# One decode pass fewer per weight tile, and new due times for W2's decode

## The chip, the cores and the metric

The kernel runs on one core of a Trainium2 chip. The metric is the time of one execution on the device in microseconds (us), as the median of several runs. Three runs of the kernel before took 1174.15, 1174.5 and 1177.13 us: median 1174.5.

## The reference

The arrays q, k and v are float32; the four weight matrices are float64. What is computed, with B = 4 batches, H = 8 heads, S = 576 positions, D = 64:

```
q, k   = rotary embedding of q, k
x      = softmax(q k^T / 8) v                      # 2304 x 512 after the heads are joined
h      = x @ w_in                                  # layer 1 (moe): 512 -> 2048
x      = (h * clip(h + 3, 0, 6) / 6) @ w_out       #                2048 -> 512
h      = x @ w_in2                                 # layer 2 (moe2): 512 -> 2048
P      = a0 + a1 h + a2 h^2 + a3 h^3
Q      = 1 + |b0| |h| + |b1| h^2
out    = (P / (Q + 1e-6)) @ w_out2                 #                2048 -> 512
```

## The kernel before

The weights of both layers arrive as 64-bit floats, seen as pairs of 32-bit integers, low word and high word (`raw`, 128 x 512 x 2). A **decode** makes one 128 x 512 float32 tile of them. There are 16 tiles for each of the four matrices: layer 1's (W1, 32 tiles, `prep_w1i` and `prep_w1o`) and layer 2's (W2, 32 tiles, `prep_w2`). A decode has these passes over 512 elements a partition: the high word, read as a float, is scaled by 2^-112, which rebases its exponent (line 557, on GpSimd or ScalarE, in the early part on VectorE or ScalarE; it shows under the helper's lines 449, 451 and 455); a shift left by 3 (L559, VectorE); the sign bit of the high word is put back in (L561, VectorE); the top bits of the low word are put in below (L565, VectorE). For the last 6 tiles of W1's first matrix the sign comes another way: ScalarE takes Sign of the high word (L564) and GpSimd multiplies by it at the end (L568).

W1's decoded tiles are bounded (Square with a sum, L582), scaled and split into two float16 parts that add up to them (lines 449 and 574). W2's decoded tiles, one `f32` buffer for all of them, are written to a scratch tensor `w2d` in device memory (L642) and read back when layer 2 begins.

**Phase 1** holds attention and layer 1. Attention works in 144 chunks of 128 queries, 36 to a batch: scores `s` (L762), their maximum `mx` (L766, scaled at L767), the exponential `e` (L772), its float16 part and residue `p` (lines 449 to 453, L779, L780), a transposing DMA to `pt` (L784), and the product with v into `ob` (L792). Each batch feeds layer 1 in two parts, with a product `h` (L859), the passes over `t` (L863, L865), the float16 parts `gh` and `gl` (L868), and the second product (L883). **Phase 2** is layer 2, in five blocks of up to 512 tokens (L1046 to L1079). It takes over the memory of attention, and then that of layer 1 and the decodes, so all W2 decodes end before its elementwise passes can begin.

The order of the instructions is the work of a **planner** (`Plan.order`). Each operation has a list of engines that may do it, a cost on each, and a due time as its priority. The planner walks through a modelled time, and at each step gives an engine that is free the ready operation with the smallest due time. A ready operation is not held back for its due time: an engine with nothing more urgent takes it. Due times are counted in ticks, one tick for a chunk. W2's 32 tiles are due evenly between `w20` and `w21`:

```
    for z in range(2 * KF):
        at(PR["w20"] + z * (PR["w21"] - PR["w20"]) / (2 * KF))
        prep_w2(z // KF, z % KF)
```

Of the kernel before, what the change touches and what calls it, by code (L numbers as in the profile page):

```python
# [10 lines left out]
F32 = mybir.dt.float32  # L11
# [4 lines left out]
AF = mybir.ActivationFunctionType  # L16
ALU = mybir.AluOpType
# [6 lines left out]
D = 64  # L24
# [6 lines left out]
KF = DFF // 128  # L31
# [7 lines left out]
PR = {'c01': -12.75,  # L39
 'e': 2,  # L40
 'e_dec': 'GA',
 'e_dec0': 'DA',
 'e_gh': 'GA',
 'e_gh0': 'AD',
 'e_gl': 'DG',
 'e_gl0': 'D',
 'e_hi': 'D',
# [118 lines left out]
 'tick': 4000,  # L166
 'u': 2,
 'vv': 1,
 'w20': 48.25,
 'w21': 163,  # L170
 'w2h': 'A',
 'w2l': 'DG',
 'wg': 4,
# [59 lines left out]
def cls(nm):  # L233
    for x in ("ob", "xu", "sm", "xt", "v9", "w0_", "w1_", "w2_", "acc"):
        if nm.startswith(x):
            return x
    return nm


def two(e):  # L240
    return float(2.0 ** e)
# [20 lines left out]
class Plan:  # L262
# [11 lines left out]
    def op(self, engs, cost, fn, r=(), w=(), lat=None, prio=None):  # L274

        o = Op()
        o.engs, o.fn, o.deps, o.idx = engs, fn, set(), len(self.ops)
        ww = [x[0] if isinstance(x, tuple) else x for x in w]; rr = [x[0] if isinstance(x, tuple) else x for x in r]
        o.nm = (">" + ww[0].tag) if ww else ("<" + rr[0].tag if rr else "?")
        o.dma = cost if type(cost) is tuple else None  # L280
        o.cost = cost if type(cost) is dict else {e: cost for e in engs}
        o.prio, o.lat = self.prio if prio is None else prio, lat
        o.prio += PR.get("o_" + cls(o.nm[1:]), 0) * 4000
        if self.first:
            o.prio += PR.get("z_" + cls(o.nm[1:]), 0) * 4000
        for writes, keys in ((False, r), (True, w)):
            for key in keys:
                t, part = key if isinstance(key, tuple) else (key, None)
                if isinstance(t, Til):
                    t.ops.append(o)  # L290
                    self.used.setdefault(t.pool, []).append(o)
                for p_, (wr, rd) in t.last.items():
                    if p_ is None or part is None or p_ == part:
                        o.deps.update(wr)
                        if writes:
                            o.deps.update(rd)
                if writes:
                    if part is None:
                        t.last.clear()
                    t.last[part] = ([o], [])  # L300
                else:
                    t.last.setdefault(part, ([], []))[1].append(o)
        o.deps.discard(o)
        self.ops.append(o)
        return o
# [99 lines left out]
def c_act(n, ap=0, sbuf=True, acc=False):  # L405
    return n / 1.2 + 51 + 42 * sbuf + 93 * ap + 190 * acc


def c_dve(n, ap=0):
    return n * 1.042 + 68 + 60 * ap  # L410


def c_dve2(n, ap=0):
    return n * 0.521 + 68 + 60 * ap


def c_copy(n, ap=0, sbuf=True):
    return {"A": c_act(n, ap, sbuf), "D": c_dve2(n, ap) if sbuf else c_dve(n, ap), "G": n * (0.9 + 0.14 * ap) + 124}


def c_sub(n):
    return {"D": c_dve(n), "G": c_pool(n)}
# [6 lines left out]
def c_pool(n):  # L429
    return n * 2.17 + 125  # L430
# [7 lines left out]
def attention_moe_moe2(ctx, tc, q, k, v, w1i, w1o, w2i, w2o, a, b, tabs, out):  # L438
# [4 lines left out]
    vec, act, pool, pe, sp = nc.vector, nc.scalar, nc.gpsimd, nc.tensor, nc.sync  # L443
    DE = {"Q": sp, "A": act}
    EL = {"D": vec, "G": pool, "A": act}

    def copy(e, out, in_, scale=1.0):
        if e == "A":
            act.activation(out, in_, AF.Copy, scale=scale)  # L449
        elif e == "G":  # L450
            pool.tensor_scalar(out, in_, scale, 0.0, ALU.mult, ALU.add)
        elif isinstance(scale, float) and scale == 1.0:
            vec.tensor_copy(out, in_)  # L453
        else:
            vec.tensor_scalar(out, in_, scale, None, ALU.mult)
    ctx.enter_context(tc.manual_schedule())
    pl = Plan()
    op, tl = pl.op, pl.tile

    def EN(key):  # L460
        return PR.get(key + "0", PR[key]) if pl.early else PR[key]
# [55 lines left out]
    def pow2(src, src_ap, n, target, nm, pool_name, inv=None, inv_ap=None):  # L517

        pi = tl(pool_name, [128, n], I32, nm + "i", 2)
        sc = tl(pool_name, [128, n], F32, nm + "s", 4)  # L520
        if inv is None:
            inv = tl(pool_name, [128, n], F32, nm + "v", 4)
            inv_ap = inv
        op("D", 75, lambda e: vec.tensor_scalar(pi(), src_ap().bitcast(I32), 1, 0x3F800000, ALU.logical_shift_right,
                                                ALU.bitwise_and), r=[src], w=[pi])
        op("D", 75, lambda e: vec.tensor_scalar(inv_ap(), pi().bitcast(F32), two(-124), two(64 - target), ALU.max,
                                                ALU.mult), r=[pi], w=[inv])
        op("D", 85, lambda e: vec.reciprocal(sc(), inv_ap()), r=[inv], w=[sc])
        return sc, inv


    def load_raw(src, is_in, f):
        t = tl("right", [128, 512, 2], I32, "raw", PR["raw"])
        w = src.bitcast(I32)

        def fn(e):
            if is_in:
                DE[e].dma_start(out=t().rearrange("p (k n) two -> p k (n two)", k=KD),
                             in_=w[:, f * 256:(f + 1) * 256].rearrange("(k p) n -> p k n", p=128))
            else:  # L540
                DE[e].dma_start(out=t().rearrange("p n two -> p (n two)"), in_=w[f * 128:(f + 1) * 128])
        op(PR["q_raw"], (450, 1456), fn, w=[t])
        return t

    def decode(t, f, sg=None):

        def lo():  # L550
            return t()[:, :, 0]

        def hi():
            return t()[:, :, 1]

        def fi():
            return f().bitcast(I32)
        op(EN("e_dec"), c_copy(512), lambda e: copy(e, f(), hi().bitcast(F32), two(-112)), r=[t], w=[f])
        op("D", c_dve2(512), lambda e: vec.tensor_single_scalar(fi(), fi(), 3, op=ALU.logical_shift_left), w=[f])  # L559
        if sg is None:  # L560
            op("D", c_dve(512), lambda e: vec.scalar_tensor_tensor(fi(), hi(), -2 ** 31, fi(), ALU.bitwise_and,  # L561
                                                                   ALU.bitwise_or), r=[t], w=[f])
        else:
            op("A", c_act(512), lambda e: act.activation(sg()[:, 0], hi().bitcast(F32), AF.Sign), r=[t], w=[(sg, 0)])  # L564
        op("D", c_dve(512), lambda e: vec.scalar_tensor_tensor(fi(), lo(), 29, fi(), ALU.logical_shift_right,  # L565
                                                               ALU.bitwise_or), r=[t], w=[f])
        if sg is not None:
            op(EN("e_sg"), c_sub(512), lambda e: EL[e].tensor_tensor(f(), f(), sg()[:, 0], ALU.mult), r=[(sg, 0)], w=[f])  # L568

    w1 = [[None] * KF for _ in range(2)]  # L570

# [5 lines left out]
    def bound(dst, dst_ap, src, n, by=1.0, src_ap=None):  # L577

        def fn(e):
            x = (src_ap or src)()  # L580
            dims = "a b c"[:2 * len(x.shape) - 3]
            act.activation(junk[:, 0:n], x.rearrange(f"p {dims} -> p ({dims})"), AF.Square, scale=by,  # L582
                           accum_out=dst_ap())
        op("A", c_act(n, 0, True, True), fn, r=[src], w=[dst])

    def total(am, am_ap, n, kind=0):
        ps, ps_ap = small(128, n, kind)
        op("P", 60, lambda e: pe.matmul(ps_ap(), lhsT=ones(), rhs=am_ap(), start=True, stop=True), r=[ones, am], w=[ps])
        return ps, ps_ap

    WG = PR["wg"]

    def prep_w1i(g):

        am = tl("right", [128, WG], F32, "wam", 2)
        fts = []
        for i in range(WG):
            raw = load_raw(w1i, True, g * WG + i)
            ft = tl("right", [128, 512], F32, f"w1_{(g * WG + i) % (KF - 1)}", 1)
            t = tl("right", [128, 2, 512], F16, f"w0_{g * WG + i}")  # L600
            w1[0][g * WG + i] = t
            decode(raw, ft, t if g * WG + i >= KF - PR["sg"] else None)
            bound((am, i), lambda i=i: am()[:, i:i + 1], ft, 512)
            fts.append(ft)
        ps, ps_ap = total(am, am, WG, 1)
        gs = slice(g * WG, g * WG + WG)
        sc, _ = pow2(ps, ps_ap, WG, 14, "wp", "right", (pwi, g), lambda: pwi()[:, gs])
        for i in range(WG):
            split16(w1[0][g * WG + i], fts[i], sc, lambda i=i: sc()[:, i:i + 1])
# [363 lines left out]
    def to_right(e):  # L973
# [15 lines left out]
       w=[(ab, 0)])  # L989
    op("Q", (450, 56), lambda e: DE[e].dma_start(out=ab()[:, 4:6], in_=b.rearrange("(o n) -> o n", o=1).to_broadcast([128, 2])),  # L990
       w=[(ab, 1)])
# [187 lines left out]
```

## Time and profile before

| What | us | Share of the span |
|---|---|---|
| median of three runs | 1174.5 | |
| the profiled execution, its time | 1176.04 | |
| the profiled execution, its span | 1174.3 | |
| TensorE (PE) busy | 978.5 | 83% |
| VectorE (DVE) busy | 1012.9 | 86% |
| ScalarE (ACT) busy | 693.6 | 59% |
| GpSimd (POOL) busy | 536.2 | 46% |

A row of a group gives the line, the engine, the operation, the tiles (out<-in, without buffer numbers), the shape and the count, then the busy time in us and the mean duration of one in ns, then the idle time of the engine just before these instructions and what ended most of it. Instructions of one engine overlap a little at their ends, so that count times mean can exceed the busy time. Names that begin with w are W1's tiles and the parts made of them, and f is the f32 buffer, which holds W2's tiles and the last tile of W1's second matrix.

### The profile page before, as it was taken

The numbers are of one execution on the slowest core, as the hardware profiler recorded it, in microseconds if no ns is written. First come the engines' busy times: TensorE is split into PE (matmuls) and PEld (weight loads), VectorE is DVE, ScalarE is ACT, GpSimd is POOL, SyncE is SP. The second block draws the span as 40 slices with busy tenths as digits, with TensorE's granted clock in tenths as the row PEclk, the third lists the DMA queues.
The fourth block names the chain that finished last, engine by engine and source line by source line (L and its number), as shares of the span: only waits on it lengthen the run. The fifth ranks groups of instructions, "written<-read, shape, count | busy, mean of one in ns | idle before, by whom it ended". The sixth has DMA issues, their size and how long they took to land.

```text
span 1174.3 us, 20041 instructions
## 1 busy us (share of the span) xinstructions
PE 978.5 (83%) x7030; PEld 756.6 (64%) x7030; DVE 1012.9 (86%) x1920; ACT 693.6 (59%) x1274; POOL 536.2 (46%) x603
## 2 busy tenths in 40 slices
PE   0222469887888889988899999989999999999997
PEld 0111247755566666666666787767888888888885
DVE  7999989799899998899978955489988887888787
ACT  5555668475455354453444526478776675676576
POOL 5799778687588857699843620035000000000000
PEclk9999989999999999899999999999999999999999
DMA  8788877787887897978869651622020020010010
GB/s 237 184 219 178 218 145 156 152 175 163 189 177 157 154 220 187 191 149 161 188 165 196 145 127 33 197 83 76 1 61 3 19 54 1 5 41 1 1 37 18
DMA packets 297445, 142.73 MB, mean 122 GB/s; under 512 B 245120, under 2 KB 278528, under 8 KB 297344
## 3 DMA queue, kind: packets, MB, share of 16 engines
q1 hardware_dynamic: 286352, 123.72, 48.8%
q10 hardware_dynamic: 10992, 17.73, 5.3%
q8 instruction: 55, 0.90, 0.3%
q14 instruction: 46, 0.38, 0.1%
HBM read 61.71 MB, written 17.83 MB: 68 GB/s over the span
## 4 chain that ended last, share of the span: by engine, by line
PE 42%; DVE 28%; DMA 8%; issue 6%; POOL 6%; ACT 4%; SPq 1%; ACTq 0%; DVEq 0%; POOLq 0%
PE ac L1079 14%; PE hh L1046 8%; PE hx L1046 7%; PE h L883 6%; PE h L859 5%; DMA pt<-p 4%; DVE mx L766 3%; DVE gl L868 2%; DVE p L453 2%; DVE t L865 2%; DMA w2d<-f 2%; DMA raw<-in_moe_w_out_dram 2%; DVE qk L732 1%; ACT e L772 1%; PE s L762 1%
## 5 line engine op out<-in xcount | busy, mean ns | idle before, releaser
L859 PE MATMUL h<-xt,w 128*128 128x256 f16 (+1 forms) x1536 | 207.6, 289 | 31.8 <-DVE t L865 27.4
L859 PEld LDWEIGHTS <-w 128*128 128x128 f16 x1536 | 149.2, 99 | 73.9 <-issue 36.9
L883 PE MATMUL h<-gh,w 128*128 128x256 f16 (+1 forms) x960 | 195.8, 290 | 0.5 <-DVE w L574 0.4
L772 ACT ACTIVATE e<-s,mx,qal 128x576 f32<-128x576 f32 x144 | 118.7, 827 | 122.8 <-DVE mx L767 37.5
L1079 PE MATMUL ac<-w,lgh 128*128 128x512 f32 x576 | 180.1, 393 | 4.8 <-ACT lgh L1069 4.0
L779 POOL TENSOR_TENSOR p<-e,p 128x512 f16<-128x512 f32 x104 | 138.9, 1335 | 64.6 <-DVE p L453 42.5
L883 PEld LDWEIGHTS <-w 128*128 128x128 f16 x1440 | 139.5, 99 | 36.3 <-DVE w L574 0.7
L883 PE MATMUL h<-gl,w 128*128 128x256 f16 (+1 forms) x480 | 139.2, 290 | 0.0
L762 PE MATMUL s<-t,t 128*128 128x512 f16 (+2 forms) x320 | 89.6, 313 | 55.1 <-ACT e L772 48.2
L792 PE MATMUL ob<-v,pt 128*128 128x130 f16 (+3 forms) x1440 | 96.3, 217 | 45.2 <-DMA pt<-p 19.3
L762 PEld LDWEIGHTS <-t 128*128 128x128 f16 (+1 forms) x640 | 59.0, 108 | 107.2 <-issue 68.4
L1079 PEld LDWEIGHTS ac<-w,lgh 128*128 128x128 f32 x576 | 106.8, 188 | 30.6 <-ACT lgh L1069 6.6
L1046 PE MATMUL hh<-x,w 128*128 128x512 f32 (+1 forms) x516 | 115.9, 373 | 2.9 <-DVE lt L1061 2.9
L792 PEld LDWEIGHTS <-pt 128*128 128x128 f16 (+1 forms) x1440 | 81.5, 105 | 55.4 <-issue 26.4
L1079 PE MATMUL ac<-w,lgl 128*128 128x512 f32 x288 | 113.6, 394 | 1.2 <-DVE lgl L1070 1.2
L766 DVE TENSOR_REDUCE mx<-s 128x1 f32<-128x576 f32 x144 | 107.0, 745 | 6.8 <-PE s L762 6.6
L1046 PEld LDWEIGHTS hh<-x,w 128*128 128x128 f32 x516 | 90.9, 188 | 23.0 <-DVE lt L1061 3.8
L1046 PE MATMUL hx<-x,w 128*128 128x512 f32 (+1 forms) x444 | 98.2, 370 | 0.0
L863 ACT ACTIVATE t<-h,half,d 128x256 f32<-128x256 f32 (+1 forms) x128 | 74.7, 585 | 26.9 <-PE h L859 25.7
L1046 PEld LDWEIGHTS hx<-x,w 128*128 128x128 f32 x444 | 77.4, 188 | 16.1
L868 DVE TENSOR_TENSOR gl<-t,gh 128x256 f16<-128x256 f32 (+1 forms) x108 | 69.2, 643 | 12.1 <-ACT gh L449 11.0
L449 ACT ACTIVATE gh<-t 128x256 f16<-128x256 f32 (+1 forms) x95 | 41.6, 440 | 51.1 <-DVE t L865 48.8
(151 smaller groups left out, 2088.8 us busy)
## 6 DMA issues: line engine op xcount, KB each, us to landing
raw<-in_moe_w_in_dram SPq DMA_DIRECT2D x32, 512.0 KB, 4.8
raw<-in_moe_w_out_dram SPq DMA_DIRECT2D x32, 512.0 KB, 4.5
w2d<-f ACTq DMA_DIRECT2D x30, 256.0 KB, 3.7
w2s<-w2d SPq DMA_DIRECT2D x22, 256.0 KB, 2.7
out_dram<-ob SPq DMA_DIRECT2D x36, 128.0 KB, 2.4
nat<-in_k_dram SPq DMA_DIRECT2D x16, 256.0 KB, 3.2
nat<-in_q_dram SPq DMA_DIRECT2D x16, 256.0 KB, 3.2
vnat<-in_v_dram SPq DMA_DIRECT2D x4, 1024.0 KB, 7.6
```

Of the source, the lines that this page charges most:

```text
L449: act.activation(out, in_, AF.Copy, scale=scale)
L762: pe.matmul(s()[r0:r0 + m, c:c + n_], lhsT=qq[:, q0:q0 + m], rhs=kk[:, k0:k0 + n_], start=(j == 0), stop=(j == 1))
L766: op("D", c_dve(576), lambda e: vec.reduce_max(mx()[:, 0:1], s()[:, 0:S], axis=AX.X), r=[s], w=[(mx, 0)])
L772: op("A", c_act(576, 2, False), lambda e: act.activation(et(), s()[:, 0:S], AF.Exp, bias=mx()[:, 1:2], scale=al()[:, 0:1]), r=[s, (mx, 1), ...
L779: EL[e].tensor_tensor(p16()[:, S + 64:2 * S], et()[:, 0:512], p16()[:, 0:512], ALU.subtract)
L792: pe.matmul(ob()[0:m, o0:o0 + c], lhsT=pt()[:, j, q0:q0 + m], rhs=v9()[:, hh, j % 5].rearrange("p s d -> p (s d)")[:, 0:c], start=(n_ == 0 ...
L859: pe.matmul(hp()[:, 0:N], lhsT=w[:, z, kk], rhs=xt()[:, kk, 0:N], start=(n == 0), stop=(n == 11))
L863: op("A", c_act(N, 2, False), lambda e, t=t, hp=hp, f=f: act.activation(t()[:, 0:N], hp()[:, 0:N], AF.Relu, bias=half(), scale=d()[:, f:f ...
L868: op(EN("e_gl"), c_sub(N), lambda e, t=t, f=f: EL[e].tensor_tensor(gl()[:, f, 0:N], t()[:, 0:N], gh()[:, f, 0:N], ALU.subtract), r=[t, (gh ...
L883: pe.matmul(yp()[:, 0:N], lhsT=w[:, s_, m * 128:(m + 1) * 128], rhs=gt()[:, f, 0:N], start=(f == 0 and z == 0), stop=(f == KF - 1 and z == 2))
L1046: pe.matmul(hp()[:, 0:n], lhsT=w[:, kk], rhs=xt()[:, kk, 0:n], start=(i == 0), stop=(i == 11))
L1079: pe.matmul(accs[j][i]()[0:m], lhsT=gt()[:, x:x + m], rhs=wt(), start=(f == 0 and z == 0), stop=(f == KF - 1 and z == 2))
```

## The change

There are two edits. First, in the decode the scaling becomes a Prelu on ScalarE in all 64 tiles. For a positive high word it scales by 2^-112 as before. For a negative one it multiplies by the slope -2^32 besides: the value turns positive, and its exponent field is larger by 32, which is the bit that the shift left by 3 then moves into the sign's place. So the pass that put the sign back (L561) is gone, and with it the other way of six tiles (L564, L568). Second, the due times of W2's decodes run from tick 112 to 165 instead of 48.25 to 163. Lines behind the decode have numbers that are 11 smaller in the changed kernel.

```
- 'w20': 48.25,
- 'w21': 163,
+ 'w20': 112.0,
+ 'w21': 165.0,
...
-    def decode(t, f, sg=None):
+    def decode(t, f):
...
-        op(EN("e_dec"), c_copy(512), lambda e: copy(e, f(), hi().bitcast(F32), two(-112)), r=[t], w=[f])
+        op("A", c_act(512), lambda e: act.activation(f(), t()[:, :, 1].bitcast(F32), AF.Prelu, scale=two(-112),
+                                                     alpha=-two(32)), r=[t], w=[f])
         op("D", c_dve2(512), lambda e: vec.tensor_single_scalar(fi(), fi(), 3, op=ALU.logical_shift_left), w=[f])
-        if sg is None:
-            op("D", c_dve(512), lambda e: vec.scalar_tensor_tensor(fi(), hi(), -2 ** 31, fi(), ALU.bitwise_and,
-                                                                   ALU.bitwise_or), r=[t], w=[f])
-        else:
-            op("A", c_act(512), lambda e: act.activation(sg()[:, 0], hi().bitcast(F32), AF.Sign), r=[t], w=[(sg, 0)])
-        op("D", c_dve(512), lambda e: vec.scalar_tensor_tensor(fi(), lo(), 29, fi(), ALU.logical_shift_right,
+        op("D", c_dve(512), lambda e: vec.scalar_tensor_tensor(fi(), t()[:, :, 0], 29, fi(), ALU.logical_shift_right,
                                                                ALU.bitwise_or), r=[t], w=[f])
-        if sg is not None:
-            op(EN("e_sg"), c_sub(512), lambda e: EL[e].tensor_tensor(f(), f(), sg()[:, 0], ALU.mult), r=[(sg, 0)], w=[f])
...
-            decode(raw, ft, t if g * WG + i >= KF - PR["sg"] else None)
+            decode(raw, ft)
```

Since the planner sees other costs, the order of all engines is new. Three places show it.

VectorE at the start of the program, the decodes of W1's first three tiles (w_0 to w_2; raw is the ring of loaded words), in the kernel before:

```order
L559 TENSOR_SCALAR w_0_109<-w_0_109 128x512
L561 SCALAR_TENSOR_TENSOR w_0_109<-raw,w_0_109 128x512
L565 SCALAR_TENSOR_TENSOR w_0_109<-raw,w_0_109 128x512
L559 TENSOR_SCALAR w_1_117<-w_1_117 128x512
L561 SCALAR_TENSOR_TENSOR w_1_117<-raw,w_1_117 128x512
L559 TENSOR_SCALAR w_2_125<-w_2_125 128x512
L565 SCALAR_TENSOR_TENSOR w_1_117<-raw,w_1_117 128x512
L561 SCALAR_TENSOR_TENSOR w_2_125<-raw,w_2_125 128x512
```

The same place in the changed kernel:

```order
L555 TENSOR_SCALAR w_0_109<-w_0_109 128x512
L556 SCALAR_TENSOR_TENSOR w_0_109<-raw,w_0_109 128x512
L555 TENSOR_SCALAR w_1_117<-w_1_117 128x512
L556 SCALAR_TENSOR_TENSOR w_1_117<-raw,w_1_117 128x512
L555 TENSOR_SCALAR w_2_127<-w_2_127 128x512
L556 SCALAR_TENSOR_TENSOR w_2_127<-raw,w_2_127 128x512
L712 TENSOR_TENSOR ropeb<-nat,tab 128x288
L713 TENSOR_TENSOR nat<-nat,tab 128x9x32
```

Two passes stand for a tile where there were three, and work of the rotary embedding follows earlier.

ScalarE in the third batch, three of W2's decodes with their writes (f is the f32 buffer, e the exponential), in the kernel before:

```order
L642 DMA w2d<-f_5634 128x512
L582 ACTIVATE junk,qam<-nat 128x576 x2
L891 DMA y1d<-t 128x320
L449 ACTIVATE f_5744<-raw 128x512
L642 DMA w2d<-f_5744 128x512
L772 ACTIVATE e<-s,mx,qal 128x576
L449 ACTIVATE t<-h,d 128x320
L449 ACTIVATE xh<-xn 128x256
L772 ACTIVATE e<-s,mx,qal 128x576
L642 DMA w2d<-f_5847 128x512
```

The same place in the changed kernel:

```order
L553 ACTIVATE f_5625<-raw 128x512
L631 DMA w2d<-f_5625 128x512
L449 ACTIVATE t<-h,d 128x320
L553 ACTIVATE f_5690<-raw 128x512
L631 DMA w2d<-f_5690 128x512
L553 ACTIVATE f_5750<-raw 128x512
L761 ACTIVATE e<-s,mx,qal 128x576
L449 ACTIVATE t<-h,d 128x320
L631 DMA w2d<-f_5750 128x512
```

All three tiles are opened on ScalarE now, where one was before in these rows, and the writes follow close behind the scalings.

VectorE at the last of W2's tiles, near the end of attention (xub and ob are the results of its chunks), in the kernel before:

```order
L804 TENSOR_REDUCE xub_79<-ob_156 64x130
L559 TENSOR_SCALAR f_9205<-f_9205 128x512
L817 TENSOR_SCALAR r<-xub_79 128x6
L453 CAST p_9241<-e 128x576
L818 RECIPROCAL r<-r 128x6
L801 TENSOR_REDUCE xub_81<-ob_261 128x65
L561 SCALAR_TENSOR_TENSOR f_9205<-raw,f_9205 128x512
L820 TENSOR_TENSOR xn<-xub_79,r 128x384
L565 SCALAR_TENSOR_TENSOR f_9205<-raw,f_9205 128x512
```

The last of W2's tiles in the changed kernel:

```order
L555 TENSOR_SCALAR f_9002<-f_9002 128x512
L755 TENSOR_REDUCE mx<-s 128x1
L854 SCALAR_TENSOR_TENSOR t<-t,h 128x256
L857 TENSOR_TENSOR gl<-t,gh 128x256
L756 TENSOR_SCALAR mx<-mx,qal 128x1
L790 TENSOR_REDUCE xub_79<-ob_155 128x65
L556 SCALAR_TENSOR_TENSOR f_9002<-raw,f_9002 128x512
L854 SCALAR_TENSOR_TENSOR t<-t,h 128x256
```

Before, the last decode stood behind the maximum (mx) of the last of 144 chunks; now the maxima of three chunks come behind it.

## Rows read from the trace of the kernel before

**Rows 1.** The page: busy us (share of the span) by engine; VectorE in 40 slices, tenths

```profile
PE 978.5 (83%) x7030; PEld 756.6 (64%) x7030; DVE 1012.9 (86%) x1920; ACT 693.6 (59%) x1274; POOL 536.2 (46%) x603
...
DVE  7999989799899998899978955489988887888787
```

**Rows 2.** Busy times by stretch: us, engines' busy time, TensorE's clock, DMA share, GB/s

```profile
0.00:167.50 167.50, 53.46 (x342) 33.24 (x343) 152.87 (x278) 98.95 (x195) 125.27 (x136) 0.98 0.86 201
167.50:690.00 522.50, 454.64 (x4334) 345.56 (x4334) 478.05 (x1006) 271.70 (x488) 382.36 (x451) 0.98 0.81 171
690.00:760.00 70.00, 70.00 (x546) 53.33 (x544) 30.79 (x60) 32.11 (x59) 1.75 (x2) 1.00 0.38 115
760.00:1174.00 414.00, 400.39 (x1819) 324.44 (x1816) 351.15 (x577) 290.84 (x532) 26.81 (x15) 1.00 0.11 29
```

**Rows 3.** TensorE's waits, 150 to 700 us: us in total, times, longest

```profile
PE h L859 <- DVE t L865: 27.4, 30, 2.6
PE s L762 <- ACT e L772: 20.6, 21, 4.1
```

**Rows 4.** ScalarE's waits, 167.5 to 690 us

```profile
ACT e L772 <- POOL mx L767: 28.5, 27, 3.9
...
ACT e L772 <- POOL p L780: 21.5, 12, 6.9
```

**Rows 5.** Pieces of the chain that ended last: start us, us, what

```profile
127.51 5.02 DMA raw<-in_moe_w_out_dram
...
704.82 26.08 PE h L859 x192
```

**Rows 6.** Groups on VectorE by form, 167.5 to 690 us

```profile
L565 DVE SCALAR_TENSOR_TENSOR f<-raw,f 128x512 int32<-128x512 int32 x32 | 27.8, 868 | 0.1
...
L561 DVE SCALAR_TENSOR_TENSOR f<-raw,f 128x512 int32<-128x512 int32 x32 | 26.0, 813 | 0.3
...
L559 DVE TENSOR_SCALAR f<-f 128x512 int32<-128x512 int32 x32 | 18.7, 585 | 8.7 <-ACT f L449 4.9 <-POOL f L451 3.9
```

**Rows 7.** Groups on VectorE, 0 to 167.5 us

```profile
L455 DVE TENSOR_SCALAR w<-raw 128x512 f32<-128x512 f32 x11 | 6.3, 575 | 0.0
```

**Rows 8.** Groups on GpSimd, whole span

```profile
L779 POOL TENSOR_TENSOR p<-e,p 128x512 f16<-128x512 f32 x104 | 138.9, 1335 | 64.6 <-DVE p L453 42.5 <-issue 10.1 <-ACT p L449 5.0
...
L780 POOL TENSOR_TENSOR p<-e,p 128x64 f16<-128x64 f32 x104 | 55.7, 536 | 0.0
...
L451 POOL TENSOR_SCALAR f<-raw 128x512 f32<-128x512 f32 x11 | 8.3, 757 | 7.6 <-DMA raw<-in_moe_w_out_dram 4.9 <-DMA w2d<-f 2.5
```

**Rows 9.** Groups on ScalarE, whole span

```profile
L772 ACT ACTIVATE e<-s,mx,qal 128x576 f32<-128x576 f32 x144 | 118.7, 827 | 122.8 <-DVE mx L767 37.5 <-POOL mx L767 34.6 <-POOL p L780 24.5
...
L582 ACT ACTIVATE junk<-w 128x512 bf16<-128x512 f32 x31 | 19.4, 626 | 29.7 <-DVE w L565 23.1 <-POOL w L568 6.3 <-ACT qk L449 0.2
...
L449 ACT ACTIVATE f<-raw 128x512 f32<-128x512 f32 x22 | 14.7, 670 | 15.1 <-DMA w2d<-f 11.7 <-DMA raw<-in_moe_w_out_dram 1.7 <-DVE t L455 1.6
```

**Rows 10.** Groups on VectorE, whole span

```profile
L453 DVE CAST p<-e 128x576 f16<-128x576 f32 x93 | 55.1, 593 | 11.2 <-DMA pt<-p 7.7 <-ACT e L772 3.3
...
L779 DVE TENSOR_TENSOR p<-e,p 128x512 f16<-128x512 f32 x40 | 35.4, 885 | 1.1 <-ACT p L449 0.6
...
L780 DVE TENSOR_TENSOR p<-e,p 128x64 f16<-128x64 f32 x40 | 15.4, 386 | 0.0
...
L574 DVE SCALAR_TENSOR_TENSOR w<-w,so,w 128x512 f16<-128x512 f32 x14 | 13.4, 956 | 0.0
...
L453 DVE CAST gh<-t 128x320 f16<-128x320 f32 (+1 forms) x15 | 7.0, 469 | 0.1
...
L453 DVE CAST xh<-xn 128x256 f16<-128x256 f32 x2 | 2.3, 1144 | 0.0
```

**Rows 11.** Busy times from 120 to 150 us, columns as in rows 2

```profile
120.00:150.00 30.00, 13.02 (x83) 7.47 (x82) 29.02 (x54) 18.63 (x38) 21.12 (x24) 1.00 0.95 221
```

**Rows 12.** Groups on VectorE, 850 to 1174 us

```profile
L1068 DVE SCALAR_TENSOR_TENSOR lt<-lq,lt 128x512 f32<-128x512 f32 (+1 forms) x66 | 41.1, 623 | 0.0
```

More of the change, by code (lines that the diff above doesn't have):

```diff
@@ L543, in load_raw @@
         return t
-    def decode(t, f, sg=None):
[L550 to L554, printed above, removed]
+    def decode(t, f):
         def fi():
             return f().bitcast(I32)
-        op(EN("e_dec"), c_copy(512), lambda e: copy(e, f(), hi().bitcast(F32), two(-112)), r=[t], w=[f])
+        op("A", c_act(512), lambda e: act.activation(f(), t()[:, :, 1].bitcast(F32), AF.Prelu, scale=two(-112),
+                                                     alpha=-two(32)), r=[t], w=[f])
         op("D", c_dve2(512), lambda e: vec.tensor_single_scalar(fi(), fi(), 3, op=ALU.logical_shift_left), w=[f])
-        if sg is None:
-            op("D", c_dve(512), lambda e: vec.scalar_tensor_tensor(fi(), hi(), -2 ** 31, fi(), ALU.bitwise_and,
-                                                                   ALU.bitwise_or), r=[t], w=[f])
-        else:
-            op("A", c_act(512), lambda e: act.activation(sg()[:, 0], hi().bitcast(F32), AF.Sign), r=[t], w=[(sg, 0)])
-        op("D", c_dve(512), lambda e: vec.scalar_tensor_tensor(fi(), lo(), 29, fi(), ALU.logical_shift_right,
+        op("D", c_dve(512), lambda e: vec.scalar_tensor_tensor(fi(), t()[:, :, 0], 29, fi(), ALU.logical_shift_right,
                                                                ALU.bitwise_or), r=[t], w=[f])
-        if sg is not None:
-            op(EN("e_sg"), c_sub(512), lambda e: EL[e].tensor_tensor(f(), f(), sg()[:, 0], ALU.mult), r=[(sg, 0)], w=[f])
     w1 = [[None] * KF for _ in range(2)]
```

## The prediction

> **What bounds the kernel now.** I read the page's busy lines first. VectorE is at 86% over the span, TensorE at 83%, and the slices of the span show VectorE at 8 and 9 tenths over its first part, before TensorE's time comes [rows 1]. The busy times by stretch make stages of that [rows 2]. Up to 167.5 us, where VectorE does its first pass of layer 1 on the output of the attention, VectorE is busy 152.87 us (91%) and TensorE 53.46. From there to 690 us VectorE has 478.05 of 522.5 us (91%) and TensorE 454.64 (87%). From 690 to 760 us TensorE is never idle, and after that it is busy 400.39 of 414 us. So phase 1 (to 690 us) is set mostly by VectorE, and the rest by TensorE.
>
> The waits say through what. Between 150 and 700 us TensorE waits 27.4 us for VectorE's pass over t and 20.6 us for ScalarE's exponential [rows 3]. The exponential itself waits for GpSimd, 28.5 us at mx and 21.5 us at the residue of p [rows 4]. In the chain of the work that ended last, 26.08 us from 704.82 on are matmuls without a gap [rows 5]: what phase 1 gives back arrives at the end of the kernel undiminished, and the matmuls themselves stay as they are.
>
> **The change, part by part.** *The sign pass.* Of the 64 decodes, 58 lose a VectorE pass: 26 in the first stretch and 32 in the second. At 813 ns [rows 6] these are 21.1 and 26.0 us. The six others lose a Sign on ScalarE and a product on GpSimd.
>
> *The scaling pass.* All 64 now open on ScalarE. VectorE loses 11 scalings at 575 ns, 6.3 us, all in the first stretch [rows 7], GpSimd 11 at 757 ns, 8.3 us [rows 8]; ScalarE gains 22. No Prelu stands in the trace. Its neighbours over the same 512 elements are Copy with 670 ns and, cheaper, the Square with 626 ns; the nearest dearer one is the exponential over 576 elements with two operands from memory, 827 ns [rows 9]. I take Copy's 670 ns, since its operands are the most alike: 14.7 us more on ScalarE, of which some 4 us go with the six Signs. Between 626 and 827 ns the 64 would cost 3 us less to 10 us more, on an engine that is busy 98.95 of 167.5 and 271.70 of 522.5 us [rows 2].
>
> *What the planner puts in its place.* Costs have changed, so every engine's order is new. VectorE ends with one instruction fewer, not 69: it takes over work of ScalarE and GpSimd. Counted in the two programs up to the first pass over t, it takes on 5 residues of p (885 + 386 ns, 6.4 us), 4 casts of p (593 ns, 2.4 us), 3 low parts of w (956 ns, 2.9 us) and 2 scalings of w, which I price like the low part (1.9 us) [rows 10]; the small rest I estimate at 2.7 us net. That makes 16.3 us against 21.1 + 6.3 = 27.4 us saved: 11 us less. Behind it come 6 residues (7.7 us), 3 casts of p (1.8 us), 12 casts of gh at 469 ns (5.6 us), and 7 casts of xh with some 15 scalings and normalisations. For xh's cast the trace has two on VectorE at 1144 ns, and gh's as the nearest other [rows 10]; I take 0.6 us, nearer to gh's since two are few, and the group comes to some 13 us. Less 4.4 us for what moved ahead of the mark that is 24 us against 26.0: only 2 us less. GpSimd loses 11 residues (1335 + 536 ns, 20.6 us), the 8.3 us of scalings, six products of about a residue's price (8 us) and small pieces, some 42 us of its 536 [rows 1, 8]. ScalarE gives away more than it gains and ends about 11 us lighter.
>
> *W2 "in the last quarter".* The numbers only set priorities, and an idle engine takes what is ready. Counted on VectorE, W2's first decode stands behind 36 chunks of attention in both programs, nine or ten are done by the 77th of 144, and the last stands behind 141 chunks instead of 144. So this half of the change hardly moves W2, and I cost it at nothing. Its cover is TensorE's full stretch from 690 us; if W2 came after that, phase 2 would wait for it. The DMA queues see the same transfers.
>
> *Sum.* In the first stretch 11 us at VectorE's 91% give 10 us. In the second 2 us come from VectorE directly, and of the 50 us that the exponential waits for GpSimd there I count 1 us, since GpSimd sheds only some 20 of its 382.36 us in it and part of that waiting is free [rows 2, 4]. Together 13 us. The profiled execution took 1176.0 us (span 1174.3), 1.5 above the median of 1174.5: 1176.0 - 13 = 1163.0, and against the median 1161.5. I say 1162.
>
> **The rivals.** *ScalarE becomes the gate (slower).* There is one f32 buffer for W2. Each decode waits in ScalarE's queue for the write of the one before (11.7 us now), and ScalarE then issues that write itself, where it stands until VectorE's two passes are done; exponentials are queued behind. For it: in the new ScalarE order 18 of 30 writes follow their scaling within three rows, before 4. With VectorE's two passes at 585 + 868 ns, 14 more such places make 20 us [rows 6], and 11 decodes that were GpSimd's add 670 ns and a wait of 690 ns (15.1 us over 22), 15 us [rows 9]. Half of these 35 us on the exponential would be 17 us; with the first stretch's 10 us gained, 1176.0 + 17 - 10 - 1.5 = 1181.5. It decides once more than 13 of the 35 us reach TensorE. Against it: ScalarE is idle half of that stretch, and the order was laid with these waits in it.
>
> *The first stretch is set by loads (no gain).* The DMA engines' share is 0.95 from 120 to 150 us [rows 11], and a wait of 5.02 us for a raw tile lies on the chain at 127.5 [rows 5]. Then shorter passes only wait for the next raw tile, and the second stretch's 3 us remain: 1171.5. Against it: over the whole stretch the share is 0.86 [rows 2], and at 0.95 throughout the same transfers would need 0.86 x 167.5 / 0.95 = 151.6 us, which leaves room for 10.
>
> *GpSimd's relief speeds VectorE (more gain).* VectorE's pass over two inputs in memory takes 868 ns in phase 1 [rows 6] and 623 ns late in phase 2, where GpSimd does nothing [rows 12]. By my estimate from the groups in rows 6 and 10 and their like, such passes, scalings and casts are some 390 of phase 1's 631 busy us. If they are a quarter too long for GpSimd's sake, that is 95 us; GpSimd's 42 fewer of 508 us take 8% off it, 8 us: 1161.5 - 8 = 1153.5.
> The Trainium skill (SBUF — State Buffer, "Who interferes with whom") has a rule for that: VectorE and GpSimd share a port pair as an exclusive lock, which VectorE's two-input passes and its casts can take. The 868 against 623 ns agrees. By that rule the casts that VectorE takes over also hold up GpSimd, which speaks against the change and makes the 8 us an upper end.
>
> **How the numbers follow.** Forecast 0.47, ScalarE as gate 0.20, loads 0.13, more gain 0.20. About 0.3%, 3.5 us, is what a measurement of this kernel can tell from no change, so faster means below 1171 and slower above 1178. Faster: 0.47 x 0.9 + 0.20 + 0.13 x 0.4, about 0.67. Same: 0.03 of the forecast's, 0.08 of the loads' and 0.02 of the gate's, 0.13. Slower: 0.18 of the gate's and 0.02 of the forecast's for ill luck with the new order, 0.20. The range goes from 1145 (more gain, with Prelu at its cheap end and the xh casts at gh's price) to 1185 (the gate, with Prelu near its dear end).
>
> **What would show it.** Right: no sign pass; VectorE's busy time lower by some 13 us, GpSimd's by some 42; the first layer-1 pass over t near 157 us instead of 167.5; 64 Prelu near 0.67 us; from the end of attention on the same distance to the end as before. Wrong: the first pass over t still near 167 us with raw tiles waited for; or ScalarE's waits for the w2d write, and for VectorE at its own issues, far above 15 us, with TensorE waiting well over 20.6 us for the exponential.

## The result, and the profile after

The changed kernel took 1163.56 us (median of 4 runs, 1162.83 to 1165.4), the kernel before on the same chip 1174.33 us: ratio 0.9905, 95% interval [0.9886, 0.9925]. The forecast was 1162. The profiled execution took 1165.4 us, its span was 1163.6.

The page of the changed kernel, busy time by engine and the slices of TensorE and of its granted clock:

```profile
PE 977.9 (84%) x7030; PEld 757.0 (65%) x7030; DVE 989.5 (85%) x1918; ACT 682.5 (59%) x1249; POOL 478.0 (41%) x560
...
PE   0214687878987989878998999989999999999997
...
PEclk9996599998999999899999999999999999999999
```

Beside [rows 1], VectorE is 23.4 us lighter, GpSimd 58.2 and ScalarE 11.1. The busy times by stretch follow, columns as in [rows 2], cut at the same marks of the changed kernel: the first and the last of layer 1's passes over t.

```profile
0.00:155.60 155.60, 54.55 (x368) 34.91 (x369) 136.65 (x262) 96.30 (x187) 100.45 (x121) 0.82 0.85 212
155.60:720.30 564.70, 494.90 (x4653) 376.96 (x4653) 486.89 (x1060) 281.92 (x506) 348.38 (x422) 0.98 0.74 162
```

And the second of these stretches in the kernel before, whose first is in [rows 2]:

```profile
167.50:731.60 564.10, 496.24 (x4681) 378.03 (x4682) 495.25 (x1044) 290.41 (x523) 382.36 (x451) 0.98 0.77 161
```

The first stretch went from 167.5 to 155.6 us, and VectorE's busy time in it from 152.87 to 136.65. The second has the same length, 564.7 against 564.1 us, although VectorE is busy 8.4 us less in it and GpSimd 34 us less. What is left to the end of the span is 443.3 against 442.7 us. So, in these two profiles, all of the gain comes from the first stretch. The chain of the changed kernel in the transition (start us, us, what) shows why it arrives at the end whole, as [rows 5] did for before:

```profile
694.95 24.61 PE h L848 x180
719.56 13.04 PE h L872 x96
```

The groups that answer to the decode, on ScalarE and VectorE of the changed kernel (the third is of 155.6 to 678.4 us):

```profile
L553 ACT ACTIVATE f<-raw 128x512 f32<-128x512 f32 x33 | 22.0, 666 | 19.7 <-DMA w2d<-f 15.2 <-DVE mx L756 4.1 <-ACT t L449 0.5
...
L553 ACT ACTIVATE w<-raw 128x512 f32<-128x512 f32 x31 | 20.2, 658 | 14.7 <-DMA raw<-in_moe_w_in_dram 8.6 <-DMA raw<-in_moe_w_out_dram 5.0 <-DVE w L563 0.9
...
L556 DVE SCALAR_TENSOR_TENSOR f<-raw,f 128x512 int32<-128x512 int32 x32 | 28.2, 883 | 0.5
```

A Prelu costs what Copy cost [rows 9]. ScalarE stands idle for 19.7 us before the 33 scalings into the f32 buffer, mostly for the write of the tile before. The waits of TensorE (138 to 690 us) and of ScalarE (155.6 to 678.4 us), to be laid beside [rows 3, 4]:

```profile
PE h L848 <- DVE t L854: 26.6, 30, 2.5
PE s L751 <- ACT e L761: 17.1, 19, 2.7
```

```profile
ACT e L761 <- DVE mx L756: 52.8, 37, 6.3
...
ACT e L761 <- POOL mx L756: 30.9, 18, 5.6
...
ACT e L761 <- POOL p L769: 16.5, 8, 5.8
```

TensorE's two waits are nearly what they were. The exponential waits longer for VectorE's mx (the page-wide row in [rows 9] has 37.5 us for before) and about as long for GpSimd.

### The profile page after: what moved, and what is told of

It reads as the page before. It is cut to its first block, busy times and chain, and to the rows that moved or that the text cites. A ratio compares the mean times of both kernels' runs of the same rounds, so it can differ in the third digit from the quotient of the medians.

```text
span 1163.6 us, 19971 instructions
## 1 busy us (share of the span) xinstructions
PE 977.9 (84%) x7030; PEld 757.0 (65%) x7030; DVE 989.5 (85%) x1918; ACT 682.5 (59%) x1249; POOL 478.0 (41%) x560
## 4 chain that ended last, share of the span: by engine, by line
PE 38%; DVE 23%; DMA 6%; issue 5%; POOL 4%; ACT 2%; SPq 1%; DVEq 0%; ACTq 0%; POOLq 0%
PE ac L1068 13%; PE hh L1035 7%; PE hx L1035 6%; PE h L872 6%; PE h L848 5%; DVE mx L755 3%; DMA pt<-p 3%; DVE p L453 2%; DVE gl L857 2%; DVE t L854 2%; DMA w2d<-f 2%; DVE lt L1057 1%; DVE lt L1055 1%; DVE qk L721 1%; DVE lgl L1059 1%
## 5 line engine op out<-in xcount | busy, mean ns | idle before, releaser
L761 ACT ACTIVATE e<-s,mx,qal 128x576 f32<-128x576 f32 x144 | 118.2, 827 | 129.8 <-DVE mx L756 52.8
L768 POOL TENSOR_TENSOR p<-e,p 128x512 f16<-128x512 f32 x93 | 118.5, 1274 | 89.5 <-DVE p L453 62.6
L751 PEld LDWEIGHTS <-t 128*128 128x128 f16 (+1 forms) x640 | 58.2, 108 | 113.3 <-issue 73.8
L857 DVE TENSOR_TENSOR gl<-t,gh 128x320 f16<-128x320 f32 (+1 forms) x109 | 68.5, 636 | 12.8 <-ACT gh L449 11.9
L453 DVE CAST p<-e 128x576 f16<-128x576 f32 x100 | 60.4, 604 | 13.6 <-DMA pt<-p 7.8
```

The lines of the kernel that those rows point to most:

```text
L751: pe.matmul(s()[r0:r0 + m, c:c + n_], lhsT=qq[:, q0:q0 + m], rhs=kk[:, k0:k0 + n_], start=(j == 0), stop=(j == 1))
L761: op("A", c_act(576, 2, False), lambda e: act.activation(et(), s()[:, 0:S], AF.Exp, bias=mx()[:, 1:2], scale=al()[:, 0:1]), r=[s, (mx, 1), ...
L768: EL[e].tensor_tensor(p16()[:, S + 64:2 * S], et()[:, 0:512], p16()[:, 0:512], ALU.subtract)
L857: op(EN("e_gl"), c_sub(N), lambda e, t=t, f=f: EL[e].tensor_tensor(gl()[:, f, 0:N], t()[:, 0:N], gh()[:, f, 0:N], ALU.subtract), r=[t, (gh ...
```

## The experiments

Each ratio is to runs of the kernel before on the same chip, whose median was 1172.43 us for the first four runs, 1171.93 or 1172.01 us for the others. Three kinds of kernel stand here: the two edits apart; the order of either kernel kept row by row and passes left out or put back; and new orders for the same work. In the profile rows the first stretch ends at the first pass over t, as above.

**The two edits apart.** The due times alone:

```
- 'w20': 48.25,  'w21': 163,
+ 'w20': 112.0,  'w21': 165.0,
```

> The kernel before with the new due times of W2 alone. Theory (the gain is the lighter decode of W1 in the first stretch): the first pass over t stays at 167 us and the time within 4 us of before, 1170 to 1178, as W2's decodes stand nearly where they stood, only the last five now behind the last maximum. Rival (the due times bring the gain): 1160 to 1167, all of it behind 230 us.

1182.7 us, ratio 1.0087 [1.0072, 1.0102]: slower, which neither side expected. The passes over t (durations, first and last start) and the shifts of the decodes on the f32 buffer in this kernel:

```profile
L865 DVE SCALAR_TENSOR_TENSOR t<-t,h x128: 368/446/490, 166.3 to 738.2; 128x256 f32<-128x256 f32 x64, 128x320 f32<-128x320 f32 x64
...
L559 DVE TENSOR_SCALAR f<-f x33: 386/427/1123, 147.5 to 717.5; 128x512 int32<-128x512 int32 x33
```

The first stretch is as before; the second has 571.9 us, 7.8 more. The last five W2 decodes now stand behind the last maximum, the last of them at 717.5 us instead of 685.3. But most of the loss arises earlier: the last maximum itself starts at 688.4 instead of 683.0 us, and from it to the last pass over t it is 49.8 instead of 48.6 us. The Prelu alone, that is the changed kernel with the old due times:

> The changed kernel with the old due times of W2. Theory: the first pass over t near 156 us and 1160 to 1167. Rival (the due times bring the gain): 1171 to 1178. Rival (the gain is luck of the new order): first pass over t anywhere from 156 to 168.

1162.2 us, ratio 0.9920 [0.9894, 0.9945].

```profile
L854 DVE SCALAR_TENSOR_TENSOR t<-t,h x128: 398/445/490, 156.8 to 717.3; 128x256 f32<-128x256 f32 x64, 128x320 f32<-128x320 f32 x64
```

This is the changed kernel's gain, most of it in the changed kernel's place: the first stretch is 10.7 us shorter than before, the second 3.6. The due times add nothing that can be told apart.

**Passes left out in the old order.** The sign pass is planned but not issued, for W1 or for W2:

```
- lambda e: vec.scalar_tensor_tensor(fi(), hi(), -2 ** 31, fi(), ALU.bitwise_and, ALU.bitwise_or)
+ lambda e: None if w1 else vec.scalar_tensor_tensor(...)        # "if not w1" for W2
```

> The order of the kernel before kept row by row, but the sign passes of W1's 26 tiles are not issued (those weights lose their sign). Theory (the first stretch is set by VectorE's sum of passes): 21 us less on VectorE, the first pass over t at 148 to 158 us, time 1155 to 1165. Rival (loads set the first stretch): first pass over t at 164 to 168, time 1171 to 1175. Rival (luck of the order): as loads, since the order is the old one.

1165.27 us, ratio 0.9937 [0.9922, 0.9953].

```profile
0.00:157.90 157.90, 53.57 (x342) 33.40 (x343) 134.55 (x253) 98.73 (x196) 117.30 (x136) 0.77 0.90 214
157.90:722.00 564.10, 495.45 (x4681) 378.00 (x4681) 495.26 (x1044) 290.03 (x523) 382.26 (x451) 0.98 0.76 161
```

VectorE sheds 18.3 us in the first stretch, which ends 9.6 us earlier, where theory had it; the second is unchanged to 0.1 us. So the sign passes alone, without a new order, bring most of the first stretch's gain, and raw tiles don't hold the stretch as a whole. But only half of what VectorE sheds arrives.

> The order of the kernel before kept row by row, but the sign passes of W2's 32 tiles are not issued (those weights lose their sign). It asks what VectorE's relief behind 167 us is worth. If VectorE's sum set that stretch: 26 us less on VectorE, time 1150 to 1155. Theory (there the waits go round between the exponential, VectorE and the transposes, and freed time mostly turns into idle time): 1166 to 1174.

1161.08 us, ratio 0.9909 [0.9893, 0.9926]: between the two expectations, so my theory that freed time turns into idle time there fell.

```profile
165.30:714.60 549.30, 490.27 (x4681) 375.83 (x4682) 471.64 (x1012) 289.36 (x523) 374.23 (x451) 0.99 0.78 166
```

23.6 us less on VectorE shorten the second stretch by 14.8, or 0.63 us for each, in these two profiles.

**Passes put back in the new order.** The sign pass is issued again in front of the last pass, for W2 or W1. It sets a bit that is already set.

```
+ vec.scalar_tensor_tensor(fi(), t()[:, :, 1], -2 ** 31, fi(), ALU.bitwise_and, ALU.bitwise_or)
  vec.scalar_tensor_tensor(fi(), t()[:, :, 0], 29, fi(), ALU.logical_shift_right, ALU.bitwise_or)
```

> The changed kernel, its order kept row by row, with the sign pass put back into W2's 32 decodes (it changes nothing in the result, as the sign is in already): 26 us more on VectorE behind 156 us. Theory A (a freed us of VectorE is worth 0.57 us there, as leaving out these passes in the old order showed, and the changed kernel's gain there went into the passes that the planner moved to VectorE): 12 to 18 us longer, 1175 to 1182. Theory B (in the new order ScalarE's waits set that stretch and VectorE's time is free): 1162 to 1168.

1188.24 us, ratio 1.013 [1.0089, 1.0171].

```profile
156.30:740.90 584.60, 498.64 (x4660) 378.07 (x4658) 509.68 (x1092) 281.81 (x506) 350.93 (x422) 0.98 0.70 157
```

22.8 us more on VectorE make the second stretch 19.9 us longer than the changed kernel's, more than the 12 to 18 of theory A. Theory B falls: VectorE's time is dear there in the new order too.

> The changed kernel, its order kept row by row, with the sign pass put back into all 32 decodes of W1 (it changes nothing in the result): some 25 us more on VectorE in the first stretch. Theory (VectorE's sum sets the first stretch): first pass over t at 168 to 180 us, 1175 to 1187. Rival (loads set it): first pass at 156 to 160, 1163 to 1168.

1183.6 us, ratio 1.0102 [1.0087, 1.0117].

```profile
0.00:175.30 175.30, 54.98 (x365) 35.28 (x366) 160.22 (x293) 96.83 (x187) 103.56 (x121) 0.82 0.76 188
```

23.6 us more on VectorE make the first stretch 19.7 us longer than the changed kernel's, as theory had it.

These prices rest on one profiled execution of each kernel, and executions of one kernel lie up to 11 us apart (1166.33 to 1177.38 us for the kernel before on one chip). By the medians, each kernel beside its own runs of before, a us of VectorE that was left out gave 0.4 us (W1) and 0.5 (W2), and one that was put back cost 0.9 (W1) and 1.2 (W2).

**ScalarE's wait for the write.** Two f32 buffers:

```
- 'f32': 1,
+ 'f32': 2,
```

> The changed kernel with two f32 buffers for W2, planned anew: a decode no longer waits in ScalarE's queue for the write just before. Theory B (those waits, 15.2 and 5.5 us in the profile of the changed kernel, set the stretch behind 156 us): that stretch shorter by 8 us or more, 1150 to 1157. Theory A (VectorE's sum sets it): within 4 us of the changed kernel, 1159 to 1167.

1162.45 us, ratio 0.9914 [0.9883, 0.9944]: the changed kernel's time, as theory A had it.

```profile
ACT f L553 <- DMA w2d<-f: 17.6, 12, 3.1
```

The planner let the decodes run further ahead (the last scaling starts at 603.4 instead of 663.7 us), so that ScalarE waits for the writes as long as with one buffer. The run therefore shows that a second buffer brings nothing; it doesn't show what the wait itself costs.

**How much the order is worth.** The passes that the planner counts are given back to it, without being issued, so that it fills nothing in:

```
  (all decodes by Prelu, old due times)
+ op("D", c_dve(512), lambda e: None, r=[t], w=[f])
```

> All 64 decodes by Prelu with the old due times, but the planner still counts a sign pass on VectorE which is not issued, so that it doesn't fill the freed time with other engines' work. Theory A: first pass over t near 157 us and the stretch behind it 10 to 15 us shorter than before: 1147 to 1155. Theory B: as the changed kernel with the old due times, 1159 to 1166.

1172.66 us, ratio 0.9993 [0.9970, 1.0017]: both theories missed.

```profile
0.00:164.30 164.30, 61.46 (x414) 39.69 (x415) 140.16 (x269) 99.51 (x196) 116.99 (x142) 0.84 0.88 210
164.30:728.00 563.70, 494.31 (x4611) 376.26 (x4608) 475.83 (x1015) 280.68 (x508) 356.11 (x429) 0.98 0.76 160
```

VectorE does 32 us less than in the kernel before up to the last pass over t, and 7.5 us less than in the changed one, and the time is that of before. An order alone can eat the whole gain. Two more orders of unchanged work, by an allowance of 84 instead of 80 ns after each operation:

```
- 'slack': 80,
+ 'slack': 84,
```

> The kernel before with the planner's allowance after an operation at 84 ns instead of 80: the same work, another order. It asks how much an order alone is worth. If orders hardly differ: within 4 us of before. If the change's gain could be luck of the order: 8 us or more away from before, to either side.

1188.98 us, ratio 1.0152 [1.0134, 1.0170]: 17 us longer with the same work, so an order alone can be worth more than the changed kernel's gain.

> The changed kernel with the planner's allowance at 84 ns instead of 80: the same work, another order. If orders hardly differ: within 4 us of the changed kernel, 1159 to 1167. If its gain is luck of the order: 1170 or more.

1169.93 us, ratio 0.9987 [0.9973, 1.0001]: 6 us longer than the changed kernel's 1163.56 on another chip, not told apart from before, and nearer to what was expected if the gain is luck of the order. So three orders with the old decode gave 1172, 1183 and 1189 us, and five with the new one 1162 to 1173: three of these are faster than before, two can't be told from it. The kernel before has the best of the three old orders. Two planned kernels side by side therefore can't show what the decode is worth; kernels with the order held can.

**The old order with the new decode.** In the first kernel the sign pass is dropped only where ScalarE opened the decode already:

```
- copy(e, f(), hi().bitcast(F32), two(-112))
+ act.activation(f(), hi().bitcast(F32), AF.Prelu, scale=two(-112), alpha=-two(32))  # if e == "A"; no sign pass then
```

> The order of the kernel before kept row by row; where ScalarE opens a decode it is a Prelu and the sign pass is not issued, where another engine opens it the sign pass stays (the result is the reference's). 41 sign passes go, 20 in the first stretch and 21 of W2's. Theory A: by the shares of the passes left out before, 20/26 of 9.7 us and 21/32 of 14.8 us, 7 and 10 us: 1152 to 1159, less than the changed kernel. Theory B: only the first stretch gains, 1163 to 1168.

1161.94 us, ratio 0.9892 [0.9842, 0.9943]: between the two expectations. The profile has the passes over t from 159.3 to 718.2 us. That is 8.2 us in the first stretch, as worked out, and 5.2 in the second, half of theory A's 10. In the second kernel all decodes open so, in the old order's place, and no sign work is issued:

> The order of the kernel before kept row by row, but all 64 decodes open with Prelu on ScalarE, and neither sign passes nor the six Signs and products are issued (the result is the reference's). VectorE loses 58 passes and 11 scalings and takes on nothing. Theory A (VectorE's sum, at the prices of the two runs that left passes out): first pass over t at 153 to 158 us, the stretch behind it 8 to 15 us shorter than before, 1147 to 1157. Rival (ScalarE is the gate once it opens all decodes in an order not made for it): 1160 to 1170.

1150.23 us, ratio 0.9806 [0.9779, 0.9833]: the fastest of all, 21.8 us below its runs of before, where the changed kernel is 10.8 below its own.

```profile
0.00:154.40 154.40, 54.44 (x340) 34.09 (x340) 123.45 (x242) 100.95 (x200) 106.97 (x130) 0.82 0.91 219
154.40:706.00 551.60, 492.51 (x4683) 376.23 (x4682) 472.96 (x1012) 295.65 (x534) 366.55 (x440) 0.99 0.80 165
```

Both stretches gain, 13.1 and 12.5 us, where VectorE sheds 29.4 and 22.3. ScalarE opens all 64 decodes here in an order that was not made for it, and is no gate.

## Why the prediction was right, and where not

*The first stretch* was right in place and nearly in size: 10 us forecast, 11.9 measured, the first pass over t at 155.6 us where about 157 was named. Leaving the passes out (9.6 us) and putting them back (19.7 us) show the cause. That the size came so near is partly luck, since two errors offset each other: VectorE shed 16.2 us instead of the 11 that I summed, and each of them brought 0.73 us instead of 0.91. The count of passes was right: at the mean durations of before, the passes that went and came make 12 us less. Beyond that, passes of the same kind were shorter, 7 us in sum (count times mean, which exceeds busy time a little). The rival with the loads falls as the gate of the whole stretch: the DMA engines went to a share of 0.90 and 0.91 when the stretch shortened in the old order, and it shortened all the same. Why only half of what VectorE sheds arrives there stays open: with the new decode in the old order it waits 13.4 us for ScalarE's scalings of W1 (5.6 before), while ScalarE's waits for raw tiles stay at 16 us in sum.

*The second stretch* is the term that was mis-sized: 2 us from VectorE and 1 us from the exponential's waits were forecast, and it came out 0.6 us longer. The 2 us were about right as a count: at the durations of before, the passes that came cost 2 us more than those that went. But VectorE shed 8.4 us there, since passes of the same kind were shorter by 10 us in sum. At the 0.63 us for one that the old order showed, that would be 5 us. What took it back is, by what is left, the new order: with the same decode, orders of this stretch had 559.5 us (slack_after, 165.6 to 725.1), 560.5, 560.9, 563.7 and 564.7 us. Which waits make the difference between them stays open. The prediction counted only GpSimd among the exponential's waits and left out the largest, VectorE's mx, with 37.5 us in the same stretch. That one rose to 52.8 us, but it doesn't sort the orders: at 560.5 us it was 32.2, at 559.5 us 46.8.

*What the planner fills in.* The step that VectorE takes over other engines' work was right in kind: over the span it is 23.4 us less busy, where 53 us of passes went (two instructions fewer by the page, where I had one). With the old order the same decode gains 22 us instead of 11. In sum the passes taken over are enough for that difference: up to the last pass over t, VectorE sheds 51.7 us for 21.8 in the old order and 24.6 us for 10.8 in the new one (by the medians), 0.42 and 0.44 us for each. By stretch it isn't so even, as the second shows, and the run with passes counted but not issued sheds 32 us and gains nothing; what the change of order costs apart from the passes isn't shown for the changed kernel.

*ScalarE as the gate* didn't come. Its waits for the write rose from 11.7 to 15.2 us, while TensorE's for the exponential fell from 20.6 to 17.1 us; it was about the size that I called too small to matter.

*GpSimd's relief* was larger than forecast (58 us, not 42). The pass that the rival named did not get shorter in the second stretch, 883 ns against 868 [rows 6], with GpSimd busy 34 us less. Others did, the residue of p for one, from 885 ns [rows 10] to 855:

```profile
L768 DVE TENSOR_TENSOR p<-e,p 128x512 f16<-128x512 f32 x45 | 38.5, 855 | 2.0 <-ACT p L449 1.7
```

Together that is the 7 and 10 us above, more than the 8 us that the rival gave, but the time did not follow. Nor is GpSimd shown to be the cause: the new decode in the old order relieves it by 18 and 16 us, and there the passes are 7 us shorter in the first stretch and 1 us longer in the second. The Trainium skill's rule (SBUF — State Buffer, "Who interferes with whom") may hold, but no gain in time from it shows here. The 868 and 623 ns are of two different passes, besides; over the whole span the former has a median of 692 ns and a longest of 1616.

*The due times* were rightly costed at nothing beside the Prelu. With the old decode they cost 10 us. The last tiles slipped behind the attention, which accounts for little of it; why the attention itself ended 5.4 us later isn't shown, and a new order alone can do as much. I had read the order of the changed kernel alone, where the last decode stands well ahead of it.

## What to carry to other kernels

When a planner lays the order anew at every edit, compare an edit with the order held first: leave the passes out, or issue the cheaper form, row by row in the old order. Here that showed 22 us for the edit, where the new plan, with passes taken over and another order, gave 11; and it gave the fastest kernel. VectorE was busy nine tenths of these stretches. In a held order it gave back about half of each us taken off it (0.4 to 0.6) and took about a whole one for each us put on (0.8 to 1.2).

## What the runs showed of the hardware that was not expected

TensorE's granted clock in the first stretch was 0.98 before and 0.82 after; the slices show 0.6 and 0.5 from 87 to 145 us, where 0.5 of full speed is the level of 1.2 GHz, after TensorE had been busy 2 and 1 tenths in the two slices ahead (2 and 2 in the kernel before, without a fall). It was as low in the old order without sign passes (0.77). No cost shows in the profile, which models the ends of matmuls: from 87.3 to 145.4 us the two 128 x 512 score products took 601 and 633 ns at a granted 0.57, and 597 and 633 ns at 1.00 in the kernel before; and the changed kernel with the old due times had 0.99 and much the same first stretch, 156.8 us. Nor does the fall belong to a kernel: of 15 executions of the kernel before on one chip, eleven had a mean clock of 0.99 over the span and four of 0.96 to 0.97, and their mean times were 1172.2 and 1172.5 us.
